# Local attention, then a feed-forward network: the second pass's weights are loaded at a closer spacing

## The chip, the cores and the metric

The kernel runs on one core of one Trainium2 chip. The metric is the time on the device in microseconds: 964.08 us, the median of three runs (962.82 to 965.86). The engines have short names: PE is TensorE, DVE VectorE, ACT ScalarE, POOL GpSimd, SP SyncE, which issues every transfer here.

## The reference

Inputs are queries, keys and values of 8 batches and 8 heads, 512 local and 32 global positions, head size 64. Local queries see the 32 global keys and the local ones at a distance of at most 32; global queries see all. The result is read as x, 4352 rows of 512, for a feed-forward network with 2048 hidden columns:

```
s_g = scale * q_g @ k_all.T                    out_g = softmax(s_g) @ v_all
s_l = [scale * q_l @ k_g.T, where(|i - j| <= 32, scale * q_l @ k_l.T, -1e9)]
out_l = softmax(s_l) @ [v_g, v_l]              x = concat(out_g, out_l), heads side by side
h = x @ w_in;  sp = log(1 + exp(h));  g = h * erf(sp);  out = g @ w_out
```

All of it is float32.

## The kernel before, in words

**Two passes.** The hidden columns are cut in two halves, one for each pass. In a pass the rows of x go by in nine chunks: chunks 0 to 7 are the 512 local rows of a batch, chunk 8 the 256 global rows. A chunk of 512 rows has eight units of 128 hidden columns. One unit is twelve matmuls into a PSUM bank h (`unit`, L896), a copy hs to SBUF that frees the bank (ACT or DVE; there are two such banks), softplus and erf on ACT for a group of four units (`gate`, L922), then on DVE or POOL the product sp, the rounded copy gh and the rest gl. The projection (`project`, L963) multiplies gh and gl by w_out into four banks op. The first pass stores its sums as `part` in DRAM, the second adds them (tiles PR) and writes the output. In the second pass chunks 2 to 7 use seven products of blocks in place of eight (`quad`, L845): they want differences of x (`seven_x`, L794, a tile T, shown as tx) and four sums of blocks of the second pass's w_in (`sums`, L750, called once for each of u = 0 and 1).

**Precision and weights.** Each float32 operand is split in a rounded high part and a rest, and a product takes three matmuls. The weights come as 64-bit words. One weight unit has two halves, and `load_w` (L636) prepares one half: a transfer of 512 KB into a tile RAW; on ACT the absolute value; on DVE three integer operations from RAW into a tile TOP (shown as top_in, top_out) and one on top of it; on ACT or DVE the copy to the high part; on DVE or POOL the rest. The second half of a unit writes the same two result tiles, and its transfer waits for the first half's last operation.

**The eight late units.** `load_late` (L1032) loads the second pass's four units of w_in (0 to 3), then the four of w_out (4 to 7). Their tiles are new ones, made of the room that attention leaves, except for units 5 to 7, which take the tiles of the first pass's w_in: unit 5 one of them (ih0), unit 6 il0 and ih1, unit 7 il1 and ih2.

**Shared buffers.** Three buffers carry the tag "raw": they hold RAW of the weights, the x loads of every chunk (shown as rx) and T of `seven_x`. One buffer has the tag "wt" and one the tag "wr": TOP of the halves a takes wt, of the halves b wr; X and Y of `sums` take wt and wr as well, and so do the tiles PR. The rounded x (xh, xl) has three buffers each, two for a chunk.

**The order of the work.** Nothing is ordered by hand. Every piece of work is added to a program with a key, the engines it may run on and an estimated duration, and `schedule` (L134) plans the order on each engine: whenever an engine comes free in its model, it takes the ready piece with the lowest key whose buffers are free, if the key lies within AHEAD = 9.043 of the lowest key that isn't done. The keys count units: chunk c of pass p starts at 4 (17 p + 2 c), so chunk 8 of the first pass at 64, the second pass at 68, its chunk 2 at 84. Units have the keys s, s + 1, ..., gates s + 5.8 and s + 9.8, projections s + 8.07 and on, x loads s - 1.8. The late weights and `sums` have keys of their own:

```python
WB0, WBS = 53.416, 3.393
load_unit(kind, src, 1, u, late[2 * i], late[2 * i + 1], WB0 + WBS * i, [ATTN])
RAW = mbuf([P, 512], I64, f"raw_{name}", "raw", 3)
load(key - RLEAD, RAW, src, 524, deps, also=[HI, LO])
TOP = mbuf([P, 512], I32, f"top_{name}", ("wt", "wr")[i % 2], 1)
X, Y = mbuf([P, 512], F32, f"sx_{u}", "wt", 1), mbuf([P, 512], F32, f"sy_{u}", "wr", 1)
sums(u, SUMS + 0.1 * u)      # SUMS = 76.0
```

The plan is made once, and on the chip each engine works through its list in that order: what waits holds up what is behind it.

Of the kernel before, what the change touches and what calls it, by code (L numbers as in the profile page):

```python
# [30 lines left out]
QLEAD, VLEAD, RLEAD, XLEAD = 0.342, 0.211, 0.14, 1.805  # L31
GOFF, POFF = 1.842, 4.066
WIN, WOUT = (-1.09, -0.66, 0.575, -0.03), (3.649, 5.434, 7.303, 2.26)
WB0, WBS = 53.416, 3.393
BIAS, AHEAD = 0.679, 9.043

SLACK, PORT = {"PE": 0.8, "SP": 0.8}, 0.7
# [1105 lines left out]
```

## Time and profile before

| | |
|---|---|
| profiled execution, its own time | 961.12 us |
| span of that execution | 959.3 us |
| PE busy | 928.4 us (97%) |
| PE weight loads busy | 772.3 us (81%) |
| DVE busy | 664.0 us (69%) |
| ACT busy | 539.3 us (56%) |
| POOL busy | 367.6 us (38%) |
| transfers | 126.67 MB, mean 132 GB/s |
| chain that ended last | PE 76%, DVE 9%, POOL 3%, DMA 2%, issue 2% |

The span runs from the first to the last instruction of one execution; the execution's own time is a little longer. A share of busy time is a mean over stages that have different limits. The chain is the work that ended last, followed back step by step to what released it. Matmuls overlap in the record: one of 512 columns shows some 390 ns, but a row of them advances by about 0.23 us each. In rows of the table by stage each engine's busy time stands with its number of instructions in brackets, in the order PE, weight loads, DVE, ACT, POOL.

### The profile page before, as it was taken

To read this page: it belongs to the slowest core of one execution; us is meant where nothing else is said; L and a number is where in the kernel's file an instruction comes from. 1 tells how busy PE (TensorE), PEld (TensorE's weight loads), DVE (VectorE), ACT (ScalarE), POOL (GpSimd) and SP (SyncE) were. 2 spreads that over 40 slices of the span, in tenths; PEclk is the share of its full clock that TensorE was granted. 3 is DMA by queue.
4 is the path that set the end of the run, shared out by engine and by line. 5 is a ranking of instruction groups with operands and counts; after the bars stand their busy time and mean duration, and the time that the engine had idled before them with its cause. 6 is when DMAs were issued, how large, how long until landed. Compare 5 with 4: busy or idle time off the path is not lost.

```text
span 959.3 us, 23505 instructions
## 1 busy us (share of the span) xinstructions
PE 928.4 (97%) x9519; PEld 772.3 (81%) x9519; DVE 664.0 (69%) x1615; ACT 539.3 (56%) x917; POOL 367.6 (38%) x289
## 2 busy tenths in 40 slices
PE   9999799999999999999999999969999999999996
PEld 7777577788777777877888888758998999899884
DVE  4999988674665656646485697898586686858442
ACT  4567576535654655456686666354465555546560
POOL 0113634132333332323353367855244444524230
PEclk9999899999999999999999999989999999999998
DMA  9778766445535555452441331204123140412203
GB/s 351 251 245 272 239 192 202 155 127 175 175 104 188 171 176 175 118 176 81 137 133 52 125 113 63 66 33 143 45 88 93 40 132 2 132 44 67 88 1 110
DMA packets 77477, 126.67 MB, mean 132 GB/s; under 512 B 11961, under 2 KB 35513, under 8 KB 77369
## 3 DMA queue, kind: packets, MB, share of 16 engines
q1 hardware_dynamic: 77368, 125.17, 41.2%
q8 instruction: 75, 1.23, 0.5%
q14 instruction: 34, 0.27, 0.1%
HBM read 98.40 MB, written 26.74 MB: 130 GB/s over the span
## 4 chain that ended last, share of the span: by engine, by line
PE 76%; DVE 9%; POOL 3%; DMA 2%; issue 2%; SPq 1%; ACT 1%; DVEq 0%; POOLq 0%; ACTq 0%
PE op L284 35%; PE h L284 31%; PE s L284 5%; DVE top_out L296 3%; PE s L285 2%; PE ga L284 2%; DVE sx L296 1%; DMA raw_out<-in_w_out_dram 1%; SPq L288 1%; DVE sm L296 1%; POOL sy L296 1%; DMA xsc<-xT 1%; DMA rx<-xsc 0%; DVE tx L296 0%; POOL sx L296 0%
## 5 line engine op out<-in xcount | busy, mean ns | idle before, releaser
L284 PE MATMUL op<-wouth,gh 128*128 128x512 f32 x544 | 217.4, 400 | 0.9 <-issue 0.9
L284 PE MATMUL op<-woutl,gh 128*128 128x512 f32 x544 | 212.5, 391 | 0.0
L284 PE MATMUL op<-wouth,gl 128*128 128x512 f32 x544 | 212.2, 390 | 0.0
L296 POOL TENSOR_TENSOR sp<-sp,hs 128x512 f32<-128x512 f32 x85 | 123.5, 1471 | 160.2 <-ACT sp L286 160.1
L284 PE MATMUL h<-xh,winh 128*128 128x512 f32 (+1 forms) x480 | 174.8, 364 | 7.8 <-ACT hs L286 7.2
L284 PE MATMUL h<-xl,winh 128*128 128x512 f32 (+1 forms) x480 | 170.8, 356 | 1.3 <-POOL xl L296 1.3
L284 PE MATMUL h<-xh,winl 128*128 128x512 f32 (+1 forms) x480 | 170.8, 356 | 0.0
L286 ACT ACTIVATE gh<-sp 128x512 fp32r<-128x512 f32 x123 | 75.0, 628 | 152.4 <-PE op L284 72.1
L296 POOL TENSOR_TENSOR gl<-sp,gh 128x512 fp32r<-128x512 f32 x60 | 87.1, 1455 | 95.6 <-ACT gh L286 53.2
L284 PEld LDWEIGHTS op<-wouth,gh 128*128 128x128 f32 x544 | 102.2, 188 | 23.4 <-issue 2.8
L284 PEld LDWEIGHTS op<-wouth,gl 128*128 128x128 f32 x544 | 102.1, 188 | 22.0
L284 PEld LDWEIGHTS op<-woutl,gh 128*128 128x128 f32 x544 | 102.4, 188 | 19.1 <-issue 0.8
L287 ACT ACT_TABLE_LOAD x90 | 115.5, 1283 | 2.3 <-PEq L1130 0.7
L296 DVE TENSOR_TENSOR gl<-sp,gh 128x512 fp32r<-128x512 f32 x76 | 86.1, 1137 | 39.0 <-ACT gh L286 33.4
L284 PEld LDWEIGHTS h<-xh,winh 128*128 128x128 f32 x480 | 91.0, 190 | 23.4 <-ACT hs L286 7.6
L296 DVE TENSOR_TENSOR hs<-h,hs 128x256 f32<-128x256 f32 x168 | 66.4, 419 | 54.2 <-PE h L284 50.4
L284 PEld LDWEIGHTS h<-xl,winh 128*128 128x128 f32 x480 | 91.2, 190 | 15.0 <-POOL xl L296 2.2
L284 PEld LDWEIGHTS h<-xh,winl 128*128 128x128 f32 x480 | 91.1, 190 | 13.2
L286 ACT ACTIVATE sp<-hs 128x512 f32<-128x512 f32 x136 | 77.1, 623 | 12.1 <-DVE hs L296 11.7
L286 ACT ACTIVATE hs<-h 128x512 f32<-128x512 f32 (+1 forms) x70 | 38.8, 556 | 73.8 <-PE h L284 72.8
L296 POOL TENSOR_TENSOR sm<-sm,mx 128x512 f32<-128x512 f32 x26 | 29.1, 1128 | 124.8 <-DVE mx L296 116.5
L296 DVE CUSTOM_DVE_ANT_0 sm<-s,cs 128x128 f32<-128x128 f32 x256 | 57.4, 285 | 26.1 <-PE s L284 25.7
(157 smaller groups left out, 1653.8 us busy)
## 6 DMA issues: line engine op xcount, KB each, us to landing
vb<-in_vB_dram SPq DMA_DIRECT2D x64, 325.0 KB, 4.2
rx<-xsc SPq DMA_DIRECT2D x30, 512.0 KB, 4.8
va<-in_vA_dram SPq DMA_DIRECT2D x64, 195.0 KB, 3.7
k<-in_kE_dram SPq DMA_DIRECT2D x32, 384.0 KB, 5.0
q<-in_qT_dram SPq DMA_DIRECT2D x32, 272.0 KB, 4.9
part<-os SPq DMA_DIRECT2D x34, 256.0 KB, 2.4
pr<-part SPq DMA_DIRECT2D x34, 256.0 KB, 2.9
out_dram<-os SPq DMA_DIRECT2D x34, 256.0 KB, 3.5
```

The lines of the kernel that those rows point to most:

```text
L284: pe = lambda n, *a, **k: pinned(nc.tensor.matmul(n, *a, **k))
L285: tr = lambda *a, **k: pinned(nc.tensor.transpose(*a, **k))
L286: act = lambda *a, **k: pinned(nc.scalar.activation(*a, **k))
L287: table = lambda name: pinned(nc.scalar.preload_act_table_set(name))
L288: dma = lambda *a, **k: pinned(nc.sync.dma_start(*a, **k))
L296: return lambda *a, **k: pinned(f(*a, **k))
```

## The change

Two constants in one line: the first key of the late units and the distance between the keys of two units that follow each other. The key of unit i is WB0 + WBS i (its second half has 0.01 more, its transfers 0.14 less).

```diff
 WIN, WOUT = (-1.09, -0.66, 0.575, -0.03), (3.649, 5.434, 7.303, 2.26)
-WB0, WBS = 53.416, 3.393
+WB0, WBS = 53.452, 2.388
 BIAS, AHEAD = 0.679, 9.043
```

The plan is made anew with these keys; all that hangs on it can change its place in an engine's list.

## Rows read from the trace of the kernel before

**Rows 1.** The page's slices: PE's busy tenths in 40 equal parts of the span.
```profile
PE   9999799999999999999999999969999999999996
```
**Rows 2.** Busy time of each engine by stage; stretch, length, then the engines.
```profile
core 0: us, PE busy (x) PEld busy (x) DVE busy (x) ACT busy (x) POOL busy (x), PEclk, DMA share, GB/s
455.00:535.00 80.00, 80.00 (x354) 66.26 (x353) 47.86 (x64) 53.99 (x86) 31.75 (x23) 1.00 0.34 112
...
560.00:605.00 45.00, 44.31 (x196) 36.19 (x194) 35.51 (x36) 32.39 (x50) 34.81 (x24) 1.00 0.26 88
605.00:645.00 40.00, 31.75 (x134) 25.34 (x135) 38.47 (x41) 16.31 (x28) 26.14 (x20) 0.94 0.17 53
645.00:665.00 20.00, 20.00 (x108) 17.37 (x107) 18.62 (x26) 9.67 (x16) 15.32 (x13) 0.94 0.43 129
665.00:905.00 240.00, 240.00 (x1508) 217.93 (x1507) 164.60 (x302) 124.61 (x206) 100.87 (x90) 1.00 0.23 72
```
**Rows 3.** Waits of PE, 540 to 700 us: total, times, longest.
```profile
PE h L284 <- ACT hs L286: 7.2, 1, 7.2
PE h L284 <- POOL xl L296: 1.3, 2, 0.9
```
**Rows 4.** The chain that ended last, in order of time: start, us, what.
```profile
529.77 2.72 PE h L284 x12
...
633.07 1.89 POOL tx L296 x2
...
637.68 4.29 DVE tx L296 x3
...
642.66 0.63 ACT gh L286
643.29 0.49 ACT hs L286
...
643.83 4.63 PE h L284 x12
648.46 6.83 PE op L284 x30
```
**Rows 5.** Instructions of DVE in order: start, us, what [idle before, what ended it].
```profile
555.67 0.76 DVE L296 CAST xh<-rx 128x512 fp32r<-128x512 f32 x2
...
603.92 1.48 DVE L296 TENSOR_SCALAR top_out<-raw_out 128x512 int32<-128x512 int32 x1 [2.74 <-POOL sx L296]
605.43 2.37 DVE L296 SCALAR_TENSOR_TENSOR top_out<-raw_out,top_out 128x512 int32<-128x512 int32 x2
...
630.39 0.69 DVE L296 TENSOR_TENSOR s2l<-sx,s2h 128x512 fp32r<-128x512 f32 x1
631.12 0.43 DVE L296 TENSOR_SCALAR top_out<-raw_out 128x512 int32<-128x512 int32 x1
631.58 1.42 DVE L296 SCALAR_TENSOR_TENSOR top_out<-raw_out,top_out 128x512 int32<-128x512 int32 x2
...
648.06 0.69 DVE L296 TENSOR_TENSOR woutl<-top_out,wouth 128x512 fp32r<-128x512 f32 x1
```
**Rows 6.** Transfers issued by SP, in order of time: start, us, what.
```profile
506.54 2.18 SPq L288 DMA_DIRECT2D rx<-xsc  x2
...
566.02 0.33 SPq L288 DMA_DIRECT2D raw_out<-in_w_out_dram  x1
...
639.30 0.35 SPq L288 DMA_DIRECT2D raw_out<-in_w_out_dram  x1
```
**Rows 7.** Instructions of POOL in order of time.
```profile
566.50 1.50 POOL L296 TENSOR_TENSOR sx<-winh 128x512 f32<-128x512 f32 x1
...
627.34 1.28 POOL L296 TENSOR_TENSOR gl<-sp,gh 128x512 fp32r<-128x512 f32 x1 [1.26 <-ACT gh L286]
```
**Rows 8.** Instructions of PE: the last h matmul of unit 2, chunk 8.
```profile
549.07 0.28 PE L284 MATMUL h<-xh,winl 128*128 128x256 f32 x1
```
**Rows 9.** The table by stage, of top_out's instructions alone: DVE, ACT, POOL.
```profile
605.00:645.00 40.00, 7.94 (x12) 0.00 (x0) 3.32 (x2) 0.94 0.17 53
```

## The prediction

> **What bounds the kernel now.** I read the slices of the page first. TensorE (PE) is busy nearly everywhere; in the second half of the span only slice 26 (623 to 647 us) stands out, with a 6 [rows 1]. The table by stage then says that between 455 and 905 us PE idles in two stretches alone: 45 - 44.31 = 0.69 us and 40 - 31.75 = 8.25 us, together 8.94 us, and that in the second of them VectorE (DVE) is busy 38.47 of 40 us [rows 2]. Elsewhere PE has no gap for an edit of this stage to give back. The waits of PE name the cause of nearly all of it: one wait of 7.2 us for the ScalarE (ACT) copy that empties a bank of h, and 1.3 us for a split of x [rows 3].
>
> The chain of waits shows what the copy waited for [rows 4]. GpSimd (POOL) starts the differences of x for chunk 2 at 633.07, DVE ends them at 641.97, then come the products of a gate, ACT's copy gh at 642.66, which stands ahead of the copy hs in ACT's order, and hs at 643.29. PE starts at 643.83, and its twelve h matmuls take 4.63 us where twelve take 2.72 us at other times: 1.91 us more. The granted clock is 0.94 in the mean of this stretch and of the next, 1.00 in the others [rows 2], and PE had been idle just before. So this place costs 7.16 + 1.91 = 9.07 us, out of 8.94 + 1.91 = 10.85 us lost in the whole second half.
>
> Why are the differences so late? They need the third of the three "raw" buffers, and that was freed only as DVE's last read of a weight half ended, at 631.58 + 1.42 = 633.00 us [rows 5]. I number the eight late units 0 to 7 (0 to 3 of w_in, 4 to 7 of w_out), with halves a and b. The half read there is 7a: its transfer was issued at 566.02 [rows 6], but its TOP tile shares the single buffer "wt" with the tile X of sums(). X of sums(0) took it at 566.50 on POOL [rows 7], X of sums(1) followed, and 7a's first operation starts at 631.12, right behind the last read of X at 630.39 [rows 5]. In the same way 6b waited for "wr" until 603.92 [rows 5]. 7b was issued at 639.30 [rows 6] and ready at 648.06 + 0.69 = 648.75 [rows 5]. The keys say why: sums() stands at 76.0 and 76.1, unit 7 at 77.2.
>
> **The change, part by part.** No instruction is added or removed; eight keys move. Unit i had 53.416 + 3.393 i and gets 53.452 + 2.388 i: 53.45, 55.84, 58.23, 60.62, 63.00, 65.39, 67.78, 70.17 in place of 53.42, 56.81, 60.20, 63.60, 66.99, 70.38, 73.77, 77.17. Key differences become time only through priority, since a transfer may go as soon as its buffers are free and its key is within 9 of the front.
>
> (a) Units 5, 6, 7 can't start earlier than now by much: they write tiles of the first pass's w_in, which the h matmuls of chunk 8 release until 549.35 us [rows 8]. But all of them now precede sums(). 7a gets "wt" when 6a lets it go, near 566 us instead of 631, and 6b and 7b get "wr" before Y of sums() does. In the stretch 605 to 645 the preparation of w_out took DVE 7.94 us [rows 9]; that leaves it. Bounds for what follows: the copy hs comes 0 to 7.94 us earlier. I take 7.94, because DVE idles only 1.5 us of 40 there [rows 2], so that what it doesn't do moves the rest forward. Then hs starts at 643.29 - 7.94 = 635.35, and is done 0.5 us later, before PE's preceding matmuls end at 643.83 - 7.16 = 636.67 [rows 3, 4]. The stall of 7.16 us goes, and with it the 1.91 us at the low clock.
>
> (b) There is a second cover. During the stall PE had nothing else to run, because the projections of chunk 0 with unit 7 (4 tiles of 6 matmuls, 24 x 0.2267 = 5.44 us by the row of 30 in 6.83 us [rows 4]) wanted 7b. Their other operands ended with a gl on POOL at 627.34 + 1.28 = 628.62 [rows 7]. With 7b ready near 590 these 5.44 us can run in the gap, whatever the copy does.
>
> (c) To make room, earlier work moves: 3b, 4a and 4b go before 535 us, where seven halves stand now. Their DVE work, about 3 us each without POOL beside them (0.43 + 1.42 + 0.69 and two conversions [rows 5]), lands where DVE is busy 47.86 of 80 us and PE loses nothing [rows 2]. Cost: 0, covered by 32 us of idle DVE; if that cover fails, at most one stall as above, 9.07 us. I take 0: that stretch is the nearest row, with seven halves and no gap. Between 535 and 585 six halves ran (3b, 4a, 5a, 6a, 4b, 5b) and six will (5, 6, 7): no difference.
>
> (d) SyncE (SP) issues the transfers in the planned order, so up to sixteen earlier issues of some 0.35 us each [rows 6] pass the x loads and the stores of partial sums. The x loads of the second pass's chunk 0 went at 506.54 us [rows 6] and were last used from 555.67 [rows 5]: over 40 us of cover. Keys 63.0 and 65.4 (units 4 and 5) stay before theirs, 66.2. Bounds: 0, and 9.45 us, the time of one half from issue to end, if one waits for a buffer until such a half is through. I take 0.
>
> What is late next: PE's two waits for xl and one for hs, 0.69 us up to 605 and 1.09 us after it. Nothing in the change speaks to them; I leave these 1.78 us in. What follows 665 us is PE without a gap for 240 us [rows 2], so a gain there moves everything behind it.
>
> Sum: 7.16 + 1.91 = 9.07 us. The profiled execution took 961.12 us (span 959.3), 2.96 us under the median of the runs, 964.08. So its own time becomes 952.05, and the median 964.08 - 9.07 = 955.0 us.
>
> **The rivals.** First, only part of it. Two shifts of DVE's operations, alone, are 0.71 us each (1.42 for two), and with POOL at work 1.19 us (2.37 for two) [rows 5]. If the excess belongs to POOL's work, which stays, the two halves give back only 2 x (0.43 + 1.42 + 0.69 + 0.42) = 5.9 us. The copy then starts at 637.4, PE at 637.9, 1.3 us of stall remain, without the clock's loss: a gain of 7.8 us, 956.3 us. If also some new gap of the size of the 1.3 us for xl comes up once or twice, 958 to 960. For it: POOL is busy 26.14 of those 40 us [rows 2]. Against it: the 5.44 us of (b) would fill that rest. The Trainium skill ("SBUF — State Buffer", section "SBUF: two separate sides") says that a DVE operation with two SBUF inputs and a GpSimd operation lock a shared pair of ports, whole instructions long, and the other one blocks. The longer rows beside POOL agree with that, and by the rule the first rival's 956.3 us would be the sum.
>
> Second, no change: the keys move but not the work. The transfers still wait for buffers, 5 to 7 for the tiles freed until 549 us, and DVE works through the same list in the same order. Then hs is as late as now: 964 us. Against it stands that "wt" and "wr" go to the lower key, and 70.2 is now below 76.
>
> Third, slower: sums() comes too late for chunk 2. Now sums(0) slips in between the halves; with the new keys all of 5 to 7 stand before it, and the first quad of chunk 2 wants its tiles. X was in use from 566.50 to 631.08 for both calls [rows 5, 7], so one takes at most 32 us. Chunk 2 began behind the row of 30 op matmuls, at 648.46 + 6.83 = 655.3 [rows 4], and with 9.07 us gained would begin at 646.2. So sums(0) may start until 614 without loss, and from 623 on the kernel is slower than before, 1 us for each us. Half 7b took 648.75 - 639.30 = 9.45 us from issue to end [rows 5, 6]; six such halves one behind another take 57 us, from the release at 549.35 [rows 8] to 606. If POOL beside them stretches them, as it stretches the shifts by 2.37 / 1.42 = 1.67 [rows 5], they take 95 us. In the middle, at 1.37, they end at 627, sums(0) at 659, and the time is 955 + 13 = 968 us. For it: DVE and POOL are both well filled from 560 on [rows 2]. Against it: halves on wt and on wr overlap, unit 5 may start before 549, and half 7b's 9.45 us hold a transfer that others hide.
>
> **How the numbers follow.** Forecast 955.0 (own range 952.5 to 957): 0.46. First rival, 956.3 to 960: 0.26. No change, 964: 0.11. Slower, about 968: 0.17. About 0.3% (2.9 us) is what a measurement here can tell from nothing. Both first cases lie beyond it but for a small tail: faster 0.70, same 0.12, slower 0.18. The range goes from 952 (all 10.85 us back, 953.2, less a us of spread) to 967, which leaves out about half of the slower case and little below.
>
> **What would show it.** In the profile of the changed kernel the last top_out operations should lie before 600 us, those of 7a directly behind 6a's, and sx of sums(0) behind both. PE's wait for hs near 636 us and the clock below 1.00 behind it should be gone, and op matmuls should stand at that place. The step (c) is wrong if PE shows a gap between 455 and 560 us; (a) is wrong if hs is still late although top_out is early, for then the gate or the differences bound DVE by themselves. The prediction fails if sums(0) ends after 646 us, or if a new gap of some us stands between 560 and 605.

## The result, and the profile after

The changed kernel takes 953.09 us, the median of four runs (951.96 to 954.61), against 964.52 us for four of the kernel before: a ratio of 0.9883, interval 0.9862 to 0.9905. The forecast was 955.0 us. The profiled execution took 953.43 us; its span is 951.6 us.

The slices of the page after, PE's busy tenths. The 6 of slice 26 [rows 1] is gone:

```profile
PE   9998799999999999999999999999999999999996
```

Busy time by stage, columns as in [rows 2] (with the stretch 535 to 560, too):

```profile
455.00:535.00 80.00, 78.79 (x349) 64.87 (x348) 59.41 (x76) 54.44 (x87) 35.66 (x25) 1.00 0.39 125
535.00:560.00 25.00, 25.00 (x157) 22.61 (x156) 15.46 (x22) 15.53 (x24) 9.38 (x8) 1.00 0.31 99
560.00:605.00 45.00, 45.00 (x200) 37.24 (x200) 34.12 (x39) 34.17 (x53) 33.35 (x24) 1.00 0.23 76
605.00:645.00 40.00, 39.50 (x175) 32.38 (x174) 35.76 (x33) 17.62 (x32) 31.47 (x22) 1.00 0.20 59
645.00:665.00 20.00, 19.65 (x119) 17.47 (x118) 14.99 (x27) 11.42 (x17) 11.29 (x9) 1.00 0.44 134
665.00:905.00 240.00, 240.00 (x1513) 218.18 (x1512) 162.56 (x301) 128.97 (x213) 101.90 (x90) 1.00 0.23 73
```

PE gains 7.75 us of busy time between 605 and 645, loses 1.21 between 455 and 535, and the clock of 0.94 is 1.00. The waits of PE, 455 to 700 us (total, times, longest), hold the whole of what is left. The ACT wait of 7.2 us [rows 3] is not among them:

```profile
PE h L284 <- DVE hs L296: 1.7, 2, 1.2
PE h L284 <- POOL xl L296: 0.4, 1, 0.4
```

The two constants act on everything from the first late transfer on, so the measure for this and for every experiment is one stretch: from the issue of that transfer to the start of PE's last row of 90 op matmuls. It holds the same 2600 matmuls in each kernel. The table by windows, columns as in [rows 2], of the kernel before and then of the changed one:

```profile
456.17:929.79 473.62, 464.67 (x2600) 407.26 (x2599) 335.77 (x507) 269.79 (x430) 226.42 (x180) 0.99 0.26 81
```

```profile
457.38:922.03 464.65, 462.59 (x2600) 406.36 (x2599) 330.13 (x504) 271.72 (x434) 227.90 (x179) 1.00 0.26 82
```

The stretch is 8.97 us shorter: PE's idle time falls from 473.62 - 464.67 = 8.95 to 2.06 us (6.89), and its busy time falls by 2.08 us with the same matmuls, mostly the rows that ran at the low clock. The forecast's sum for this was 9.07 us.

Where the 7.16 us had stood, the changed kernel runs 24 op matmuls. PE's timeline shows them, from the wait for hs ahead of them to the next bank of h:

```profile
634.39 0.50 PE L284 MATMUL h<-xh,winh 128*128 128x512 f32 x1 [0.50 <-DVE hs L296]
...
637.25 0.39 PE L284 MATMUL op<-wouth,gh 128*128 128x512 f32 x1
...
642.69 0.39 PE L284 MATMUL h<-xh,winh 128*128 128x512 f32 x1
```

ACT's timeline in the same place, of the changed kernel and then of the kernel before. The copy hs that PE had waited for starts at 638.88, against 643.20 (the 643.29 of [rows 4]), and sits again behind gh. Counted from the first late transfer that is 181.50 us in place of 187.03:

```profile
637.82 1.15 ACT L286 ACTIVATE gh<-sp 128x512 fp32r<-128x512 f32 x2 [5.75 <-POOL sp L296]
638.88 0.58 ACT L286 ACTIVATE hs<-h 128x512 f32<-128x512 f32 x1
```

```profile
643.20 0.58 ACT L286 ACTIVATE hs<-h 128x512 f32<-128x512 f32 x1
```

So the copy is still late: both banks are full at 637.25, and without the 24 matmuls PE would idle until about 639.

The weight halves that had come last are earlier. DVE's timeline: the first operation of 7a (631.12 in [rows 5]), of 6b (603.92) and of 7b:

```profile
562.93 0.42 DVE L296 TENSOR_SCALAR top_out<-raw_out 128x512 int32<-128x512 int32 x1
...
575.06 1.51 DVE L296 TENSOR_SCALAR top_out<-raw_out 128x512 int32<-128x512 int32 x1
...
603.61 1.50 DVE L296 TENSOR_SCALAR top_out<-raw_out 128x512 int32<-128x512 int32 x1 [2.74 <-POOL sx L296]
```

SP issues the last weight transfer, that of 7b, at 568.74 in place of 639.30 [rows 6]:

```profile
568.74 0.33 SPq L288 DMA_DIRECT2D raw_out<-in_w_out_dram  x1
```

On POOL, X of sums() now begins behind 7a (566.50 before [rows 7]), Y directly behind the last read of wr by 6b, and 7b's rest ends at 609.49 + 1.67 = 611.16 us:

```profile
577.69 1.73 POOL L296 TENSOR_TENSOR sx<-winh 128x512 f32<-128x512 f32 x1
...
582.51 1.30 POOL L296 TENSOR_TENSOR sy<-winl 128x512 f32<-128x512 f32 x1 [3.09 <-DVE woutl L296]
...
609.49 1.67 POOL L296 TENSOR_TENSOR woutl<-top_out,wouth 128x512 fp32r<-128x512 f32 x1 [3.23 <-DVE wouth L296]
```

The table of top_out's instructions alone (DVE, ACT, POOL). 7b is the half that is left here, about where 6b had been (603.61 against 603.92 [rows 5]); DVE spends 4.37 us less on w_out than in [rows 9]:

```profile
605.00:645.00 40.00, 3.57 (x5) 0.00 (x0) 1.67 (x1) 1.00 0.20 59
```

### The profile page after: what moved, and what is told of

Read it like the earlier page. It is cut to its first block, busy times and chain, and to the rows that moved or that the text cites. A ratio compares the mean times of both kernels' runs of the same rounds, so it can differ in the third digit from the quotient of the medians.

```text
span 951.6 us, 23498 instructions
## 1 busy us (share of the span) xinstructions
PE 925.8 (97%) x9519; PEld 771.3 (81%) x9519; DVE 656.3 (69%) x1612; ACT 541.4 (57%) x921; POOL 368.8 (39%) x288
## 4 chain that ended last, share of the span: by engine, by line
PE 82%; DVE 7%; POOL 5%; DMA 3%; issue 3%; ACT 1%; SPq 0%; DVEq 0%; POOLq 0%
PE op L284 35%; PE h L284 32%; PE s L284 6%; PE s L285 3%; PE ga L284 3%; DVE top_out L296 2%; PE spare L284 2%; DVE top_in L296 1%; POOL sp L296 1%; DMA k<-in_kE_dram 1%; POOL sx L296 1%; POOL sy L296 1%; DMA vb<-in_vB_dram 1%; DMA raw_out<-in_w_out_dram 1%; PE ga L285 1%
## 5 line engine op out<-in xcount | busy, mean ns | idle before, releaser
L296 POOL TENSOR_TENSOR gl<-sp,gh 128x512 fp32r<-128x512 f32 x55 | 81.2, 1480 | 90.8 <-ACT gh L286 48.7
L296 DVE TENSOR_TENSOR gl<-sp,gh 128x512 fp32r<-128x512 f32 x81 | 90.4, 1122 | 36.3 <-ACT gh L286 33.4
```

The lines of the kernel that those rows point to most:

```text
L296: return lambda *a, **k: pinned(f(*a, **k))
```

## The experiments

The theory after this reading: the 9 us come from two things in one place, room on DVE (the copy hs is earlier) and cover (op matmuls stand between two fills of the banks). Rivals: room alone does it; cover alone does it; or it is a matter of which units move, early or late ones. The table holds every run; "stretch" is the one defined above, idle is its length less PE's busy time, and the ratio is to runs of the kernel before in the same set (medians 964.52, 964.03, 963.27 or 963.14 us). Stretch, idle and busy come from one profiled execution each; the two of the changed kernel differ by 0.15 us.

| run | what is in it | median us | ratio, interval | stretch | idle | busy |
|---|---|---|---|---|---|---|
| before | | 964.52 | | 473.62 | 8.95 | 464.67 |
| after | all eight keys | 953.09 | 0.9883 (0.9862 to 0.9905) | 464.65 | 2.06 | 462.59 |
| after_again | the same kernel | 952.79 | 0.9895 (0.9861 to 0.9930) | 464.50 | 1.93 | 462.57 |
| e1_out_old | new keys for units 0 to 3 | 965.33 | 1.0019 (1.0005 to 1.0034) | 475.30 | 10.20 | 465.10 |
| f3_u567 | for units 5 to 7 | 959.38 | 0.9953 (0.9937 to 0.9969) | 468.36 | 3.61 | 464.75 |
| g3_cover | before, chunk 0 frees its op early | 961.15 | 0.9976 (0.9958 to 0.9993) | 470.81 | 5.41 | 465.40 |
| g5_late2_5 | after, cover taken away | 956.27 | 0.9927 (0.9903 to 0.9951) | 468.01 | 3.79 | 464.22 |
| e2_in_old | for units 4 to 7 | 963.05 | 0.9987 (0.9974 to 1.0000) | 473.27 | 9.27 | 464.00 |
| f7_u34 | for units 3 and 4 | 961.37 | 0.9970 (0.9953 to 0.9986) | 472.32 | 5.91 | 466.41 |
| f5_own | before, own X and Y | 960.82 | 0.9974 (0.9953 to 0.9995) | 471.07 | 6.10 | 464.97 |
| h5_out_new_own | units 4 to 7, own X and Y | 957.28 | 0.9938 (0.9919 to 0.9958) | 468.92 | 3.44 | 465.48 |
| e9_wbs19 | spacing 1.9 | 955.70 | 0.9914 (0.9892 to 0.9936) | 465.90 | 2.95 | 462.95 |
| e6_after_sums78 | after, sums() at 78 | 957.86 | 0.9937 (0.9915 to 0.9960) | 469.15 | 5.10 | 464.05 |
| h8_after_sums77 | after, sums() at 77 | 953.07 | 0.9887 (0.9851 to 0.9923) | 464.08 | 1.46 | 462.62 |

**Cover without room.** In the kernel before, chunk 0 of the second pass reads unit 6's tiles where it wants unit 7's, so that its last projections needn't wait for 7b; it leaves out unit 7's weights there, though unit 7 is still prepared in full.

```diff
-            WH, WL = W["out", ps, u]
+            WH, WL = W["out", ps, 2 if (ps, c, u) == (1, 0, 3) else u]
 ...   # the same choice in the line that tells the plan what is read
```

> The kernel before, in which the second pass's chunk 0 reads unit 6's tiles where it should read unit 7's; unit 7 is still loaded and prepared at its old place, only nobody in chunk 0 waits for it, so the 24 op matmuls can stand between the last two h of chunk 1. DVE's order is the old one. Cover alone: the copy hs still comes at about 643.2 us, but 5.44 us of the wait are filled: some 1.7 us of stall, no low clock, a gain of 7.3 us: 957 us. Rival 'only DVE's room counts': the stall stays, 964 us.

The wait at the old place falls from 7.16 to 1.78 us. PE's timeline, at that place:

```profile
647.50 0.50 PE L284 MATMUL h<-xh,winh 128*128 128x512 f32 x1 [1.78 <-ACT hs L286]
```

But the twelve h matmuls behind it take 4.45 us (to 651.95) at a low clock. The table by windows of 5 us, clock in the third column from the end:

```profile
645.00:650.00 5.00, 3.22 (x12) 2.24 (x11) 4.78 (x7) 3.44 (x7) 1.62 (x2) 0.84 0.32 127
650.00:655.00 5.00, 5.00 (x20) 4.03 (x19) 3.45 (x6) 3.31 (x6) 0.00 (x0) 0.82 0.24 60
```

And the waits of PE (455 to 700 us) show what came next. DVE is as late as before, so chunk 2 finds its xl not split:

```profile
PE h L284 <- POOL xl L296: 2.2, 3, 1.1
PE h L284 <- ACT hs L286: 1.8, 1, 1.8
PE h L284 <- DVE hs L296: 1.3, 2, 0.8
```

The stretch gains 2.81 us, where 7.3 were expected. Cover alone moves a part of the loss to the start of chunk 2.

**Room without cover.** In the changed kernel the projections of chunk 0 with unit 7 get a later key, so that they stand behind the h matmuls again.

```diff
-                add({"PE": 1.37}, at(i), lambda t=t, u=u: mm2(t, u), ...
+                add({"PE": 1.37}, at(i) + (LATE7 if (ps, c, u) == (1, 0, 3) else 0), lambda t=t, u=u: mm2(t, u), ...   # LATE7 = 2.5
```

> The changed kernel, in which the projections of the second pass's chunk 0 with unit 7 get a key 2.5 higher, so that PE does them behind chunk 1's last h, as before the change; the order of DVE stays that of the changed kernel. Room alone: the banks of h are full at 637.1 us and the copy hs ends at 639.5, so a wait of 2 to 2.5 us shows and the time is 955 to 956 us. If only the cover counted, the stall would be back whole: 960 to 962 us. If only room counted, no change: 953 us.

PE waits for the copy again, 2.08 us, and the twelve matmuls behind it take 4.18 us. PE's timeline and then the windows around it:

```profile
637.01 0.50 PE L285 MATMUL h<-xh,winh 128*128 128x512 f32 x1 [2.08 <-ACT hs L287]
```

```profile
635.00:640.00 5.00, 2.99 (x10) 2.38 (x11) 2.40 (x2) 3.76 (x8) 2.76 (x3) 0.84 0.12 46
640.00:645.00 5.00, 5.00 (x20) 4.03 (x19) 3.54 (x8) 4.92 (x7) 2.50 (x3) 0.82 0.00 0
```

The stretch is 468.01 us, 3.36 us above that of the changed kernel: 2.08 of wait and 4.18 - 2.72 = 1.46 of slow matmuls make 3.54. Counted from the first late transfer, PE's restart moves from 643.83 - 456.17 = 187.66 to 637.01 - 454.94 = 182.07 us, so the copy comes 5.59 us earlier than before. Room is worth 5.61 us of the stretch, cover the other 3.36, and each is needed for the whole.

**Which units.** The early ones alone (0 to 3), then 5 to 7 alone:

```diff
-WB0, WBS = 53.416, 3.393
+WBK = (53.452, 55.84, 58.228, 60.616, 66.988, 70.381, 73.774, 77.167)     # e1_out_old
+WBK = (53.416, 56.809, 60.202, 63.595, 66.988, 65.392, 67.78, 70.168)     # f3_u567
-        load_unit(kind, src, 1, u, late[2 * i], late[2 * i + 1], WB0 + WBS * i, [ATTN])
+        load_unit(kind, src, 1, u, late[2 * i], late[2 * i + 1], WBK[i], [ATTN])
```

> Units 0 to 3 (w_in) get the new keys, units 4 to 7 (w_out) keep the old ones. Theory 'unit 7 in time' (the gain comes from w_out's last unit being ready before PE runs out of work near 636 us): the halves of 4 to 7 stay where they were, so the stall of 7.2 us stays: 964 us, ratio 1.00. Rival 'w_in earlier' (the gain comes from the w_in halves leaving the crowded stretch): about 955 us, ratio 0.99.

> Units 0 to 4 keep the old keys, units 5, 6, 7 get the new ones. Theory 'unit 7 in time': 7a comes before sums(0) and 7b behind it, as in the changed kernel, so most of the gain is there: 954 to 957 us, no wait of several us near 636. Rival 'room' (3b, 4a and 4b have to leave the stretch after 535 us, or DVE is late all the same): 960 to 965 us.

The early units alone leave the big wait as it was (PE's timeline of e1_out_old) and add a wait of 1.2 us near 501 us; the stretch is 1.68 us longer than before:

```profile
645.95 0.79 PE L284 MATMUL h<-xh,winh 128*128 128x512 f32 x1 [7.16 <-ACT hs L286]
```

Units 5 to 7 alone take the wait away, but gain 5.26 us of 8.97. Counted from the first late transfer, 7b starts at 616.04 - 460.85 = 155.19 us there, 8.96 us later than in the changed kernel (603.61 - 457.38 = 146.23); sums() ends after it, and PE waits for xl as chunk 2 begins. The waits of PE in f3_u567, 455 to 700 us:

```profile
PE h L284 <- POOL xl L296: 1.4, 3, 1.0
PE h L284 <- DVE xl L296: 1.0, 2, 0.7
PE h L284 <- DVE hs L296: 0.8, 1, 0.8
```

So the new keys of units 0 to 4 are worth 3.71 us on top of those of 5 to 7, although by themselves those of 0 to 3 cost 1.68 us and those of 3 and 4 gain only 1.30 (below).

**A miss: units 4 to 7.** With all four units of w_out at the new keys (63.004, 65.392, 67.78, 70.168) and those of w_in at the old ones, I expected most of the gain.

> Units 0 to 3 keep the old keys, units 4 to 7 (w_out) get the new ones: the counterpart of the run with the new keys on w_in alone, which gained nothing. Cover (unit 7's op matmuls between chunk 1's last two h) and room (4a and 4b before 535 us) are both there, and the wait of 1.2 us for hs near 501 us, which came with the new w_in keys, should be gone: 951 to 953.5 us, ratio 0.987 to 0.989. If the w_in keys carry a share of the gain beside these: 956 us or more.

There was next to none. In place of the 7.16 us for ACT stands one wait of 9.27 us for DVE. PE's timeline and DVE's:

```profile
629.76 0.80 PE L284 MATMUL h<-xh,winh 128*128 128x512 f32 x1 [9.27 <-DVE hs L296]
```

```profile
620.62 0.43 DVE L296 TENSOR_SCALAR top_out<-raw_out 128x512 int32<-128x512 int32 x1 [4.25 <-POOL sx L296]
...
629.03 0.68 DVE L296 COPY hs<-h 128x512 f32<-128x512 f32 x1
```

PE's bank had been full since 620.49 us (629.76 - 9.27) at the latest, and the copy hs was to free it. But it stood on DVE's list behind halves of w_out, which waited for the buffers of X and Y while POOL worked through sums(): DVE idled 4.25 us ahead of the first of them, and was busy only 25.26 of the 40 us from 605 to 645. To test that reading, X and Y got buffers of their own, once in this kernel and once in the kernel before, where the same buffers had made 7a wait:

```diff
-        X, Y = mbuf([P, 512], F32, f"sx_{u}", "wt", 1), mbuf([P, 512], F32, f"sy_{u}", "wr", 1)
+        X, Y = mbuf([P, 512], F32, f"sx_{u}", "sumx", 1), mbuf([P, 512], F32, f"sy_{u}", "sumy", 1)
```

> New keys for units 4 to 7 alone, as in the run that gained nothing (963 us, a wait of 9.3 us for hs on DVE, which stood behind 6b and 7b, which waited for wr behind a chain of sums() on POOL); here X and Y of sums() have buffers of their own, so 6b goes before sums() and 7b into its first part. If the halves that wait behind sums() were what stopped DVE's list: the 9.3 us go, 953 to 956 us. If the new w_in keys are needed by themselves: 960 us or more.

> The kernel before with its old keys, but X and Y of sums() have two buffers of their own in place of wt and wr, so that no half waits for sums(). By the plan 6b and 7a go ahead of most of sums(), 7b in its midst, and unit 7's op matmuls stand between chunk 1's last two h. If the shared pair is what held unit 7 back: 956 to 959 us (cover whole, room in part, as with new keys for 5 to 7 alone, 959.4). If the keys matter by themselves: 962 to 965 us.

With units 4 to 7 the 9.27 us are gone, and the stretch falls by 4.35 us; the shared buffers were the cause of the long wait. A shorter one, for x's split on DVE, takes a part of its place, and the time stays above the 953 to 956 us expected. Most of what is lacking against the changed kernel is PE's busy time, 465.48 us against 462.59, with a granted clock of 0.91 in the mean from 605 to 645. PE's timeline of h5_out_new_own:

```profile
605.88 0.79 PE L284 MATMUL h<-xl,winh 128*128 128x512 f32 x1 [2.58 <-DVE xl L296]
```

With the old keys the free buffers gain 2.55 us only, and the time lies between the two expected. 7a no longer waits for X, but the halves now come in a heap: DVE is busy without a break from 559.23 us on, nearly all of it with them, each pair of their operations takes 3.37 us, and a copy hs stands behind them. PE's timeline of f5_own, then DVE's:

```profile
573.44 0.80 PE L284 MATMUL h<-xh,winh 128*128 128x512 f32 x1 [4.72 <-DVE hs L296]
```

```profile
565.61 3.37 DVE L296 SCALAR_TENSOR_TENSOR top_out<-raw_out,top_out 128x512 int32<-128x512 int32 x2
...
572.70 0.68 DVE L296 COPY hs<-h 128x512 f32<-128x512 f32 x1
```

**Units 3 and 4 alone.** Their keys are 60.616 and 63.004, the others' old.

> Only units 3 and 4 get their new keys; 5, 6, 7 keep the old ones. 3b, 4a and 4b leave the stretch behind 535 us, but sums() still goes before 6b and 7a, and unit 7's op matmuls stay behind chunk 1's last h. Theory 'cover and room at its end': 7a and 7b still sit on DVE near 620 to 640 us, so most of the stall stays: 961 to 964 us. Rival 'room anywhere' (what matters is only how many halves are done before 535 us): 955 to 957 us.

The stretch gains 1.30 us. The projections wait for w_out now (DVE wouth 1.4, DVE woutl 1.8, POOL woutl 1.5 us), and the clock is lower than before in two stages (0.96 from 605 to 645, 0.91 from 645 to 665): PE's busy time is the longest of all runs, 466.41 us.

**When is sums() too late, and is closer still better?** In the changed kernel SUMS = 76.0 becomes 78.0 or 77.0; or the spacing becomes 1.9 from 53.416 on. The changed kernel ran beside them once more.

> The changed kernel with the key of sums() at 78: nearly all of sums(0) and sums(1) comes behind all halves, tx and the first output of chunk 0. The forecast's third rival said that each us by which sums() ends after chunk 2 wants it costs a us: if chunk 2's first products wait for s tiles, 956 to 966 us and PE waits for s there; if sums() has slack enough, 952 to 955 us.

> The changed kernel with the key of sums() at 77 in place of 76: 7b too stands before sums(0), and sums(1) moves behind the first tx. Room and cover as in the changed kernel: 952 to 955 us. If the later sums() holds up chunk 2 or DVE's list: 956 us and more.

> Spacing 1.9 from 53.416: all sixteen halves stand before most of sums(). What the changed kernel still loses in this half of the span is 1.2 us near 501 and 0.9 us later, so there is little left to win: 951 to 954 us if the closer spacing jams nothing; above 956 us if the earlier halves delay the gates of the first pass's last chunks.

> The changed kernel once more, as the measure for the three others of this set: 952 to 955 us.

At 78 the third rival's loss appears: DVE goes on with the second call of sums(), begun on POOL at 617.88, only at 639.15 us, behind the first output of chunk 0 (os), for which it idles 4.95 us. The split of the differences of chunk 2 and a copy hs then come late. DVE's timeline and PE's:

```profile
638.42 0.69 DVE L296 TENSOR_TENSOR os<-op,pr 128x512 f32<-128x512 f32 x1 [4.95 <-PE op L284]
639.15 0.69 DVE L296 TENSOR_TENSOR sy<-winl 128x512 f32<-128x512 f32 x1
```

```profile
654.00 0.39 PE L284 MATMUL h<-xl,s1h 128*128 128x256 f32 x1 [1.19 <-DVE xl L296]
659.00 0.43 PE L284 MATMUL h<-xh,winh 128*128 128x256 f32 x1 [2.69 <-DVE hs L296]
```

The stretch is 4.50 us longer than that of the changed kernel. At 77 the time is that of the changed kernel, 953.07 us. The spacing 1.9 has two waits for xl near 606 and 608, 1.7 us together, and is not better. No version beats the changed kernel by more than the runs can tell.

## Why the prediction was right

**Place and sum.** The loss named was the one that went: 8.97 us in the stretch against 9.07. The medians differ by more, 11.4 us in the first set and 10.35 beside after_again. The interval of the second (0.9861 to 0.9930, 6.7 to 13.4 us) contains 8.97, that of the first (9.2 to 13.3 us) just does not. The profiled executions don't show where 1.4 to 2.4 us more would lie: ahead of the first late transfer, where PE runs the same list, the two of the changed kernel take longer than that of the kernel before (457.38 and 456.87 against 456.17), and those of the various kernels issue the transfer anywhere from 454.94 (g5_late2_5) to 460.85 us (f3_u567). Whether these microseconds are more than the spread of the runs stays open.

**(a) Room was mis-sized.** I took 7.94 us, all of the DVE time spent on w_out in that stretch. But 1.03 us of it stood behind the copy and could not hold it up. The table of top_out's instructions (DVE, ACT, POOL) in the kernel before, cut at the copy's start:

```profile
605.00:643.20 38.20, 6.90 (x10) 0.00 (x0) 3.32 (x2) 0.96 0.18 55
643.20:645.00 1.80, 1.03 (x2) 0.00 (x0) 0.00 (x0) 0.50 0.00 1
```

And 7b stayed there with 3.57 us [rows 9 against after], so that the copy moved by 5.59 us (g5_late2_5). The stall alone would have gone from 7.16 to 2.08 us, and most of the loss at the low clock would have stayed. This is nearly the first rival's arithmetic (5.9 us for two halves and 1.3 us of stall), except that it let the loss at the low clock go.

With SUMS = 77 all of w_out has left the stretch, 7b too. The copy starts at 637.24 - 457.14 = 180.10 us from the first late transfer, 6.93 us earlier than before. The table of top_out's instructions and ACT's timeline of h8_after_sums77:

```profile
605.00:645.00 40.00, 0.00 (x0) 0.00 (x0) 0.00 (x0) 1.00 0.16 46
```

```profile
637.24 0.58 ACT L286 ACTIVATE hs<-h 128x512 f32<-128x512 f32 x1
```

The 6.90 us of w_out that stood ahead of the copy thus moved it by about as much, although the pieces of sums() changed their places there, too. That agrees with the mechanism of (a), that DVE's work moved the rest forward; what failed was its size, with the order for 7b below as the main reason. Even then the copy falls just short of the 7.16 us of the stall.

In the changed kernel DVE's woutl of half 7a took 1.66 us while POOL worked (sp from 565.24 to 568.12), that of 6b 0.69 us while POOL idled. That agrees with the lock that the Trainium skill describes ("SBUF — State Buffer", section "SBUF: two separate sides"). No run here took POOL's work away, so what these longer operations cost the copy is not shown.

**(b) Cover paid for the rest.** It was written as a second safety for a stall that (a) had already removed. In fact it was needed: the 24 matmuls lie at 637.25 to 642.69, and without them 3.36 us come back. Its own price was right, 5.44 us of matmuls for a hole of about 2. (The 0.2267 us for one matmul is that of the row of twelve in 2.72 us; the row of 30 named for it gives 0.2277.)

**(c) Not free, but cheap.** The forecast took 0, with a bound of 9.07, and named a gap between 455 and 560 us as the sign of being wrong. The changed kernel waits 1.21 us at 502.28 for a copy hs behind two operations of a w_in half on DVE, and e1_out_old shows that loss alone (1.68 us of stretch). That DVE had 32 us idle in those 80 us was no cover, since the copy stands in a list. PE's timeline in the changed kernel and then DVE's:

```profile
502.28 0.50 PE L284 MATMUL h<-xh,winh 128*128 128x512 f32 x1 [1.21 <-DVE hs L296]
```

```profile
498.26 3.37 DVE L296 SCALAR_TENSOR_TENSOR top_in<-raw_in,top_in 128x512 int32<-128x512 int32 x2
...
501.55 0.68 DVE L296 COPY hs<-h 128x512 f32<-128x512 f32 x1
```

**(d) Right at 0.** SP issues the second x load of chunk 0 only at 531.55 us, but DVE begins to round it at 558.39, so 26.84 us of cover are left; PE waits for nothing from it.

**The order.** "All of 5 to 7 precede sums()" held for 7a and 6b. It failed for 7b, forecast for about 590 and ready at 611.16: Y took wr on POOL at 582.51, right behind 6b, while the first operation of 7b needs DVE. A lower key wins within one engine's list, and here another engine reached the buffer first. With SUMS = 77 DVE's timeline has the forecast order (7b from 582.81 to 587.07, Y of sums() behind it), and the time is the same, so with the cover in place this cost nothing.

**What was left in.** 1.78 us of small waits became 0.85 us (0.50 for hs, 0.35 for xl), and 1.21 new ones of (c) came in. The errors cancel: the small waits' 0.93 us make up for most of (c). That 9.07 came out as 8.97 is therefore in part luck: (a) alone fell 3.36 us short of the changed kernel, and (b), counted only as a second safety, made that up.

**The rivals.** "No change" and "slower" fell, but both of their mechanisms exist near by. e2_in_old has the same keys for w_out and no gain; e6_after_sums78 needs only a step of 2 in one key to lose half of it. Its price, 4.5 us, is a third of the 13 us by which the third rival put its time above 955.

## What to carry to other kernels

Where each engine works through a fixed list, ask of every wait for a shared buffer what stands behind it on that list: the loss appeared here as a wait for ACT (7.16 us), for DVE (9.27) or, smaller, for a split of x (2.58), according to what happened to be behind. That an engine is idle for much of a stretch is no cover for an instruction in the middle of its list. And price room (work that leaves an engine) and cover (other work for the waiting engine) apart, with the next wait that each would meet; here either one alone left a third to two thirds of the loss.

## What the runs showed of the hardware that I had not expected

Short waits of PE cost the clock loss of the long one. From the start of the first to the start of the matmul behind them, twelve h matmuls took 4.46 us behind the wait of 7.16 us (643.83 to 648.29; the 4.63 us of [rows 4] go to the end of the twelfth). Behind 1.78 us (g3_cover) they took 4.45, and behind 2.08 us (g5_late2_5) 4.18, in place of 2.72. The granted clock of 0.82 to 0.84 in those windows of 5 us is a mean of its two levels, 1.00 (2.4 GHz) and 0.50 (1.2 GHz). PE's waits of about 2 us were followed by the lower one, here in g3_cover and then in g5_late2_5 (columns as in [rows 2]):

```profile
649.00:651.00 2.00, 2.00 (x6) 1.52 (x5) 1.90 (x2) 1.25 (x4) 0.89 (x1) 0.50 0.00 0
```

```profile
639.00:641.00 2.00, 2.00 (x6) 1.55 (x5) 0.00 (x0) 1.97 (x4) 0.00 (x0) 0.50 0.00 0
```

In the kernel before the clock was at 0.50 already from 643.20 on (the table in (a)), while PE still waited, so a part of the low clock cost nothing there. Behind the wait of 1.21 us in the changed kernel twelve took 2.89 us (502.28 to 505.17), in a stage with a clock of 1.00. What a wait of 2 us cost was thus near 3.5 us, and a price for a wait can't be read off its length alone. The first rival's stall of 1.3 us without any loss of clock lies between that wait of 1.21 us and one of 1.50 us in f7_u34 (at 652.19, with a clock of 0.91 in the mean from 645 to 665), and no run here decides it.
